# A gated attention block on one core: one table for all engines' orders, banks and places, in place of a recorded schedule that was rearranged

## The chip, the core and the metric

The kernel runs on one core of a Trainium2 chip. Its time is the device time of one execution in microseconds (us); a version is told by the median of its runs. The core's engines run side by side, each through its own list of instructions in order: PE multiplies matrices (PEld loads its weights), ACT computes functions such as the exponential, DVE and POOL compute elementwise, SP issues DMA transfers. ACT and POOL can issue transfers too. An instruction can wait for a semaphore, which other instructions or landed transfers raise; whatever stands behind it on its engine waits with it.

## The reference, cut to what matters

All in bf16; S = 2048 rows, D = 448, 16 heads of 28, F = 1792. The input B_x isn't used.

```python
xn = _layernorm(x)                       # x: (1, 2048, 448)
qkv = xn @ wqkv                          # to q, k, v of (16 heads, 2048, 28)
p = softmax(q @ k.T * 28 ** -0.5)        # for each head, 2048 x 2048
s = (p @ v) @ wo                         # (2048, 448)
g = silu(gelu(xn @ w1 + b1) @ w2 + b2)   # F = 1792 inside
return x + s * g
```

## The kernel before

**Tiles and stages.** The 2048 queries are cut into C = 4 chunks of 512, the heads into G = 4 groups of four; a group's four heads lie in four strips of 32 partitions. A pair of group and chunk is a block (16 of them). In a block, each of 16 tiles of 128 keys gives four score tiles of 128 x 512, one a head, 1024 in all (`qT,kT` in the profile, f32 in a bank of PSUM; the eight banks are the `ring`). A score tile is made into exponentials in one of two ways. ACT takes two or three banks at once through Exp (`P<-ring`, or to places in `h` or `xnT` that are free at the time). Or DVE writes an approximation by integer arithmetic (one pass to uint16 from the bank) and two further terms, which are the first one shifted by a constant (`H` on DVE, two halves `G` on POOL). PE then multiplies the exponentials with V (`P,vaug` and the like), 32 partitions a head, and adds up over the keys in one bank; in the approximate way, each of the terms is multiplied by its own scaled V, and sometimes two shifted terms are added first (on DVE, or by an accumulating DMA that POOL issues) so that PE has one matmul less for each tile. A column of ones in V gives the softmax's sums. At a block's end DVE takes the bank out (`E_sb`), and the reciprocals of the sums make a round trip through DRAM on SP's queue (`rs`, `recs`, then `x_sb<-recs`, the broadcast). Between the score tiles PE does the projections (`xnT,wq`, `xnT,wk`, `wv,xnT`), the MLP (`xnT,w`, `w,h`) and the output. The tail multiplies by g, adds to the copy of x in `out`.

**The start.** `loads` (L1378) issues on SP: x of chunk 0, its first tile alone and then its second (semaphores s_x0t, s_x0), two pieces of wq/wk for head group 0, tiles 1 to 3 of chunk 1 of x (s_x1), wv in two pieces (s_wv), chunks 2 and 3 of x, the remaining columns of wq/wk in four pieces, w1 in two; then two copies of x into `out` (`out_x`), wo, b1, and much later w2 and b2. ACT's queue issues tiles 2 and 3 of chunk 0, two pieces of wq/wk and tile 0 of chunk 1, 448 KB together. Chunk 0 is normalised on DVE and ACT (`p_ln`, `p_ln2`), turned on PE (`ident,h`), projected to q and k (`p_first`), and V of chunk 0 is made in `p_v0` (L1921, 64 matmuls `wv,xnT`), whose last 28 a hook puts behind the first four scores. `p_warm` has PE multiply `E_sb,ident` without use until the scores start; `p_busy` with `filler` (L1720) later adds products with a zero matrix to the bank of the sums where the planner finds PE idle.

**What sets the order.** `schedule` plays all these tasks in a planner in Python with costs and due times; each is recorded as an operation with its needs (`op`, L324). `arrange` (L441) then joins some shifted terms or gives some groups of exponentials from ACT to DVE (`TO`), and takes for PE, ACT, DVE and POOL the operations in an order that the table `ORD` gives as distances. For SP it has no entry: SP keeps the recorded order. `place` gives some turns of a bank another bank (`BANKS`) and derives the waits that follow; `emit_all` (L553) numbers the semaphores and issues waits and operations, an operation's waits one by one. All instructions pass through one line of the helper `_Eng`, so in the profile nearly all show L258 (L381 in the changed kernel), and are told apart by their tiles.

Of the kernel before, what the change touches and what calls it, by code (L numbers as in the profile page):

```python
# [6 lines left out]
dt = mybir.dt  # L7
# [7 lines left out]
ORD = {  # L15
# [39 lines left out]
    ),  # L55
    'ACT': (
# [8 lines left out]
    ),  # L65
    'DVE': (
# [21 lines left out]
TO = ()  # L88
# [10 lines left out]
H = 16  # L99
# [198 lines left out]
class _Kernel:  # L298
# [58 lines left out]
    def add(self, t, need, name):  # L357
# [5 lines left out]
        o.no = name  # L363
        return o

    def to(self, ms, us, at, engines, n, ports):


        K = self
# [2663 lines left out]
```

## Time and profile before

| | |
|---|---|
| median of 3 runs | 410.63 us (409.8 to 410.68) |
| span of the profiled execution | 408.0 us |
| busy PE / ACT / DVE / POOL | 395.1 / 398.1 / 343.5 / 194.8 us |
| mean granted clock of PE | 0.998 |
| first exponential on ACT | 12.58 us |
| end of ACT's last computation | 405.50 us |
| moved by DMA | 17.54 MB |

The page gives no time of the profiled execution other than its span, from the first instruction to the last; the runs' times also hold what lies around it. Rows of a timeline are: start, time from the first start to the last end of the group, engine, line, operation, tiles out<-in, shape, count, and in brackets the idle time before it and what ended that. In the rows by stage stand, behind the stage's length, the busy time and count of PE, PEld, DVE, ACT and POOL, then the granted clock, the mean busy share of the sixteen DMA engines and GB/s. Rows of transfers: tiles, issuing queue, count, KB each, median us from issue to landing.

### The profile page before, as it was taken

What the parts mean: (1) busy time and instruction counts of PE and PEld (TensorE: products, weight loads), DVE (VectorE), ACT (ScalarE), POOL (GpSimd) and SP (SyncE); (2) the same over time, 40 slices, a digit from 0 to 9 for tenths busy, and PEclk for the clock granted to TensorE, in tenths of its full rate; (3) what the DMA queues carried; (4) which work ended last, traced back from release to release, by engine and by line L of the source; (5) the groups of instructions that cost most, each with busy time, mean ns of one, the idle gap of its engine ahead of it and who ended that gap; (6) DMA issues with size and microseconds to landing.
All of it is one profiled execution on the core that took longest, in us unless ns stands there. A gap on an engine that the chain in (4) does not pass through costs nothing.

```text
span 408.0 us, 14601 instructions
## 1 busy us (share of the span) xinstructions
PE 395.1 (97%) x6157; PEld 144.6 (35%) x6157; DVE 343.5 (84%) x596; ACT 398.1 (98%) x409; POOL 194.8 (48%) x221
## 2 busy tenths in 40 slices
PE   6899999999999999999999999999999999999996
PEld 5443233333332333332223444332333323333363
DVE  8967688896679889989898127999998999798976
ACT  5999999999999999999999999999999999999995
POOL 7595457649982563254652231156156013555041
PEclk9999999999999999999999999999999999999999
DMA  8902110000101010100331100220010003200065
GB/s 244 305 2 42 4 31 2 16 20 19 29 3 31 2 25 11 34 2 2 77 116 30 30 3 6 55 53 15 18 34 2 4 31 57 64 20 21 14 114 134
DMA packets 18783, 17.54 MB, mean 43 GB/s; under 512 B 8941, under 2 KB 15421, under 8 KB 18686
## 3 DMA queue, kind: packets, MB, share of 16 engines
q1 hardware_dynamic: 16734, 13.55, 12.0%
q0 software_dynamic: 1008, 2.49, 3.8%
q8 instruction: 48, 0.79, 0.9%
q10 hardware_dynamic: 976, 0.57, 0.5%
q14 instruction: 17, 0.14, 0.1%
HBM read 12.54 MB, written 2.88 MB: 38 GB/s over the span
## 4 chain that ended last, share of the span: by engine, by line
PE 59%; ACT 28%; issue 7%; DVE 4%; DMA 1%; POOL 0%; ACTq 0%; DVEq 0%; POOLq 0%
PE ring L258 59%; ACT P L258 16%; ACT h L258 8%; ACT xnT L258 3%; DVE st L258 1%; DVE h L258 1%; DVE xnT L258 1%; DMA x_sb<-in_A_x_dram 1%; DVE vaug L258 0%; DVE x_sb L258 0%; ACT w L258 0%; DVE qT L258 0%; POOL h L258 0%; DVE mv L258 0%; DVE w L258 0%
## 5 line engine op out<-in xcount | busy, mean ns | idle before, releaser
L258 ACT ACTIVATE P<-ring 128x1024 bf16<-128x1024 f32 (+1 forms) x236 | 253.8, 1246 | 1.0 <-PE ring L258 1.0
L258 PE MATMUL ring<-qT,kT 32*128 32x512 bf16 (+2 forms) x1131 | 131.7, 359 | 4.2 <-ACT P L258 1.0
L258 ACT ACTIVATE h<-ring 128x1024 bf16<-128x1024 f32 (+2 forms) x93 | 101.3, 1204 | 2.0 <-PE ring L258 2.0
L258 PEld LDWEIGHTS ring<-qT,kT 32*128 32x128 bf16 x1131 | 36.3, 91 | 121.8 <-ACT P L258 48.1
L258 DVE TENSOR_SCALAR vaug<-ring 128x512 uint16<-128x512 f32 x92 | 60.8, 683 | 5.5 <-PE ring L258 4.8
L258 PE MATMUL ring<-xnT,w 128*32 128x512 bf16 (+1 forms) x880 | 65.3, 381 | 0.0
L258 PE MATMUL ring<-w,h 128*32 128x448 bf16 x896 | 58.5, 356 | 0.0
L258 PE MATMUL ring<-P,vaug 128*32 128x512 bf16 (+2 forms) x606 | 57.9, 351 | 0.2
L258 POOL TENSOR_TENSOR qT<-x_sb,E_sb 128x512 bf16<-128x512 f32 x15 | 17.4, 1162 | 64.6 <-DMA x_sb<-recs 38.0
L258 ACT ACTIVATE xnT<-ring 128x1024 bf16<-128x1024 f32 (+2 forms) x41 | 47.6, 1199 | 0.5 <-PE ring L258 0.5
L258 POOL TENSOR_TENSOR rc<-rs,mone 128x16 f32<-128x16 bf16 x11 | 33.3, 3023 | 28.7 <-DMA rs<-E_sb 14.6
L258 DVE TENSOR_SCALAR w<-ring 128x512 uint16<-128x512 f32 x52 | 34.5, 683 | 2.0 <-PE ring L258 1.7
L258 PEld LDWEIGHTS ring<-xnT,w 128*32 128x32 bf16 (+1 forms) x880 | 21.7, 96 | 28.0 <-issue 6.6
L258 PEld LDWEIGHTS ring<-w,h 128*32 128x32 bf16 x896 | 19.3, 95 | 24.4 <-issue 14.8
L258 PE MATMUL ring<-h,vaug 128*32 128x512 bf16 x201 | 25.1, 383 | 0.0
L258 PE MATMUL ring<-xnT,wq 128*32 128x512 bf16 (+2 forms) x240 | 22.6, 379 | 0.2 <-DVE w L258 0.2
L258 PEld LDWEIGHTS ring<-P,vaug 128*32 128x32 bf16 x606 | 17.3, 95 | 13.6 <-issue 7.4
L258 PE MATMUL ring<-xnT,wk 128*32 128x512 bf16 (+2 forms) x244 | 21.8, 379 | 0.3 <-DVE xnT L258 0.2
L258 DVE TENSOR_SCALAR h<-ring 128x512 uint16<-128x512 f32 x28 | 18.9, 685 | 3.3 <-PE ring L258 3.0
L258 POOL TENSOR_TENSOR qsq<-qT 128x512 bf16<-128x512 bf16 x12 | 13.0, 1079 | 17.0 <-DVE x_sb L258 13.9
L258 DVE CAST qT<-ring 128x512 bf16<-128x512 f32 x15 | 10.3, 688 | 12.7 <-PE ring L258 12.7
L258 DVE CAST h<-ring 128x512 bf16<-128x512 f32 x24 | 16.5, 688 | 4.8 <-PE ring L258 4.8
(207 smaller groups left out, 616.8 us busy)
## 6 DMA issues: line engine op xcount, KB each, us to landing
x_sb<-recs SPq DMA_DIRECT2D x60, 64.0 KB, 2.1
w<-in_B_w_dram SPq DMA_DIRECT2D x1, 1568.0 KB, 7.3
w<-in_B_w_dram SPq DMA_DIRECT2D x1, 1344.0 KB, 8.7
x_sb<-in_A_x_dram SPq DMA_DIRECT2D x2, 448.0 KB, 6.6
out_dram<-in_A_x_dram SPq DMA_DIRECT2D x2, 448.0 KB, 10.6
out_dram<-h POOLq DMA_DIRECT2D x4, 224.0 KB, 4.6
out_dram<-h SPq DMA_DIRECT2D x7, 112.0 KB, 4.4
xnT<-wq POOLq DMA_DIRECT2D x1, 512.0 KB, 6.6
```

Of the source, the lines that this page charges most:

```text
L258: return lambda *a, **k: f(*[real(x) for x in a], **{n: real(x) for n, x in k.items()})
```

## The change

`ORD`, `TO` and `BANKS` go. A string `PLAN` of 3541 entries holds one order over all engines, SP among them, and with each entry the places it uses: `S5/5` is score tile 5 in bank 5, `X0,1/0,1` is an Exp of tiles 0 and 1 into cells 0 and 1, `A` a pass of DVE's approximation with its unit, `H`/`G` a shift on DVE or POOL, `V` a product with V, `E` the taking out of a block's bank, `P`, `J`, `Q` the parts and the end of a projection, `C` a score tile from a padded copy of q, `R16` the recorded operation number 16 as it is (loads, norms, output), with the banks of its turns. `arrange` drops the filler and the recorded scores, exponentials, products with V and projections, and makes them anew in the table's order; each gets its waits from who wrote or read its bank, cell or unit last. The cells of one Exp can now lie at a stride. The entry `M`, an addition of two shifted terms, exists, and the table has none: the five additions of before (two on DVE, three as DMAs of POOL) are left out, and PE multiplies both terms.

```diff
-ORD = {
-    'PE': (
...
-BANKS = {
...
+PLAN = """
+    R16 R29 R250 R21 R2 R3 R4 R5 R6 R7 R8 R0 R1 R9 R22 R27 R30 R17 R33 R264 R38 R24 R34 R28 R294 R31 R25 R35/6 R32 R36/6 R37/6 R39/6 R18 R40/6 R41/6
...
+    R128 R131 R110/4 R132 R262 R97 R119/4 R116/7 R121/7 R112 R136 R127/7 S0/0 S1/1 S5/5 S3/3 S2/2 R137/6 R129 X0,1/0,1 R124 S4/4 R147/6 S7/1 S6/0
...
 class _Use:
+        self.pos = list(range(base, base + n))
...
     def get(self):
-        i = self.use.base + self.off if self.off is not None else slice(self.use.base, self.use.base + self.use.n)
+        p = self.use.pos
+        i = p[self.off] if self.off is not None else slice(p[0], p[-1] + 1, p[1] - p[0] if len(p) > 1 else 1)
...
     def arrange(self):
-        seq = {}
-        for x in TO:
-            (self.to if len(x) > 2 else self.join)(*x)
-        self.chain_up()
...
-            for d in ORD.get(name, ()):
-                at.append(left.pop(d))
-            seq[E] = [lst[i] for i in at + left]
-        self.place(seq)
-        self.emit_all(seq)
+        K = self
+        K.number()
...
+            if name(o) == "filler.f" or o.kind == "x" or name(o) == "p_expq" and s is None:
+                return "gone"
...
+        plan = [(x[0], *([int(z) for z in y.split(",") if z] for y in x[1:].split("/"))) for x in PLAN.split()]
...
+        for x in plan:
+            t, a, at = x[0], x[1], x[2] if len(x) > 2 else []
+            if t in "SC":
+                o = score(a[0], at[0], t == "C")
+            elif t == "X":
+                bs = [sc[m][1] for m in a]
+                st = bs[1] - bs[0] if len(bs) > 1 else 1
+                src, dst = K.ring[:, bs[0]:bs[-1] + 1:st, :], cells(at)
+                need = [("R", H(sc[m][0])) for m in a]
+                for c in at:
+                    need += room([K.b_P[c]], cell, c)
...
+            elif t == "V":
...
+                if m0 in grouped:
+                    need += [("R", H(p)) for p in ([ap[m0 + k] for k in range(4)] if i == 0 else sh[m0, i][1])]
...
     def emit_all(self, seq):
...
+                most = {}
                 for kind, (s, c) in o.need:
...
                         done[id(p.sem)] = p.cnt
-                        self.prog[E].append(lambda eng, s=p.sem, c=p.cnt: eng.wait_ge(s, c))
+                        most[id(p.sem)] = p
+                for p in most.values():
+                    self.prog[E].append(lambda eng, s=p.sem, c=p.cnt: eng.wait_ge(s, c))
```

What that makes of the two orders that the prediction speaks of most is shown here, a row for each instruction or run of like ones: line, operation, tile out<-tile in, shape, and how many.

SP's queue of before at the start of the program; x_sb and h hold the loaded x and wq/wk, a shape of 128x448 is one tile of 112 KB, 128x1792 a chunk of 448 KB:

```order
L258 DMA x_sb<-in_A_x_dram 128x448 x2
L258 DMA h<-in_A_wqkv_dram 128x2x112
L258 DMA h<-in_A_wqkv_dram 64x2x112
L258 DMA x_sb<-in_A_x_dram 128x1344
L258 DMA wv<-in_A_wqkv_dram 128x3x448
L258 DMA wv<-in_A_wqkv_dram 64x448
L258 DMA x_sb<-in_A_x_dram 128x1792 x2
L258 DMA h<-in_A_wqkv_dram 128x2x336 x3
L258 DMA h<-in_A_wqkv_dram 64x2x336
L258 DMA w1<-in_B_w1_dram 128x3x1792
L258 DMA w1<-in_B_w1_dram 64x1792
L258 DMA out_0_dram<-in_A_x_dram 16x14336 x2
```

SP's queue of the changed kernel, from its sixth load on; the five ahead of these are one tile of x (112 KB), 168 KB of wq/wk, a copy of 448 KB of x to out, and 56 and 28 KB of wq/wk:

```order
L381 DMA x_sb<-in_A_x_dram 128x1792
L381 DMA h<-in_A_wqkv_dram 128x2x336
L381 DMA x_sb<-in_A_x_dram 128x448
L381 DMA w1<-in_B_w1_dram 128x3x1792
L381 DMA x_sb<-in_A_x_dram 128x1344
L381 DMA w1<-in_B_w1_dram 64x1792
L381 DMA x_sb<-in_A_x_dram 128x1792
L381 DMA b1h<-in_B_b1_dram 128x14x1
L381 DMA h<-in_A_wqkv_dram 128x2x336
L381 DMA wv<-in_A_wqkv_dram 128x3x448
L381 DMA h<-in_A_wqkv_dram 64x2x336
L381 DMA wv<-in_A_wqkv_dram 64x448
```

wv moved from the sixth and seventh load to the 15th and 17th, x's tiles 1 to 3 of chunk 1 (128x1344) from the fifth to the tenth, w1's large piece (1344 KB) from the 14th to the ninth, and one copy to out from the end to the third place.

PE of before around the first scores (qT,kT); xnT,wk and qsq,bsel belong to k and q of chunk 0, wv,xnT to its V:

```order
L258 MATMUL ring<-xnT,wk 128x256 x2
L258 MATMUL ring<-qsq,bsel 128x256
L258 MATMUL ring<-xnT,wk 128x256 x2
L258 MATMUL ring<-qsq,bsel 128x256
L258 MATMUL ring<-wv,xnT 32x112 x36
L258 MATMUL ring<-qT,kT 128x512 x4
L258 MATMUL ring<-wv,xnT 32x112 x28
L258 MATMUL ring<-qT,kT 128x512 x2
```

and PE of the changed kernel at that place:

```order
L381 MATMUL ring<-xnT,wq 128x256 x4
L381 MATMUL ring<-csq,bsel 128x1
L381 MATMUL ring<-xnT,wk 128x256 x4
L381 MATMUL ring<-qsq,bsel 128x256 x2
L381 MATMUL ring<-wv,xnT 32x112 x64
L381 MATMUL ring<-qT,kT 128x512 x5
```

The V projection's 28 matmuls that followed the first four scores now stand ahead of all scores, with the other 36.

More of the change, by code (lines that the diff above doesn't have):

```diff
@@ L336, in op @@
         o.sem, o.cnt = h if h else (None, 0)
+        if spec and spec[0] in ("exp", "a", "h", "evac", "last"):
+            for b in writes:
+                self.first_w.setdefault(id(b), ([b.w] if b.w is not None else []) + [x for x in b.r if x is not None])
         o.need = [("X", x) for x in self.pre[E]]
@@ L441, in arrange @@
-    def arrange(self):
-        seq = {}
-        for x in TO:
-            (self.to if len(x) > 2 else self.join)(*x)
-        self.chain_up()
-        for E, name in ((PE, "PE"), (ACT, "ACT"), (DVE, "DVE"), (POOL, "POOL"), (SP, "SP")):
-            lst = [o for o in self.ops if o.E == E]
-            at, left = [], list(range(len(lst)))
-            for d in ORD.get(name, ()):
-                at.append(left.pop(d))
-            seq[E] = [lst[i] for i in at + left]
-        self.place(seq)
-        self.emit_all(seq)
@@ L542, in chain_up @@
-    def chain_up(self):
-        chain = [o for o in self.ops if o.port and o.start is not None]
-        for at, o in sorted(self.put_port[::-1], key=lambda x: -x[0]):
-            chain.insert(at, o)
-        last = {}
-        for o in chain:
-            for E, kind in ((POOL if o.E == DVE else DVE, "P"), (o.E, "Q")):
-                if E in last:
-                    o.need.append((kind, (last[E].sem, last[E].cnt)))
-            last[o.E] = o
+        of = lambda h: K.by_h[(id(h[0]), h[1])]
@@ new lines, in arrange @@
+        kd = {id(o): kind(o) for o in K.ops}
+        writer, unit_at, opens = {}, {}, {}
+        for o in K.ops:
+            if o.spec and o.spec[0] in ("s", "sc", "pv"):
+                for b, (_, h) in zip(o.rd, [x for x in o.need if x[0] == "R"]):
+                    if kd[id(of(h))] in ("rest", "ev"):
+                        writer.setdefault(id(b), {})[(id(h[0]), h[1])] = h
+            if o.spec and o.spec[0] == "h":
+                unit_at.setdefault(o.spec[1], {}).update({o.spec[5]: o.spec[2], o.spec[4]: 0})
@@ new lines, in arrange @@
+        final = {o.spec[1]: o for o in K.ops if o.spec and o.spec[0] == "last"}
+        plan = [(x[0], *([int(z) for z in y.split(",") if z] for y in x[1:].split("/"))) for x in PLAN.split()]
+        ops, seq = {o.no: o for o in K.ops}, {E: [] for E in (PE, ACT, DVE, POOL, SP)}
+        full = {x[1][0] for x in plan if x[0] == "P" and x[1][1] == KT - 1}
+        merged = {x[1][0] for x in plan if x[0] == "M"}
+        grouped = {x[1][0] // 4 * 4 for x in plan if x[0] == "A"}
+        left = [sum(1 for x in plan if x[0] == "V" and x[1][0] // 64 == b) for b in range(NBLK)]
@@ new lines, in through @@
+        def through(p):
+            c, s = kd[id(p)], p.spec
+            if c == "rest" or c == "ev":
+                return [p]
+            if c == "pr":
+                return [evac[s[1]]]
+            if c == "core" and s[0] == "last":
+                return [p]
+            if c == "core" and s[0] in ("s", "sc", "pv"):
+                b = (s[1] if s[0] != "pv" else s[2][0])[0] // 64
+                return [final[b]] if b in final else []
+            return []
+        was = {id(o): list(o.need) for o in K.ops}
@@ new lines, in arrange @@
+        K.ops = [o for o in K.ops if kd[id(o)] == "rest" or o in list(evac.values()) or o in list(final.values())]
+        bank = {i: [] for i in range(NRING)}
+        cell, lane = {}, {}
+        sc, ex, ap, sh, pads, acc, burst, begun, part = {}, {}, {}, {}, {}, {}, {}, {}, set()
+        pr, done, last_pad, port, e1 = {}, set(), [], None, None
+        pad_of = [o for o in K.ops if name(o) == "p_pad" and o.E == SP]
+        shc = [o for o in K.ops if name(o) == "p_pad.f"][0]
+        vs = {o.spec[1:]: o for o in K.ops if o.spec and o.spec[0] == "vs"}
@@ new lines, in new, with take, cells @@
+        def new(E, fn, need, spec, port=False):
+            K.n_new += 1
+            o = K.op(E, fn, (K.evsem[E], 10 ** 6 + K.n_new), 1, (), (), "t", 0.1, 0.05, "", (), port, spec=spec)
+            o.need += need
+            return o
+        def take(i):
+            need = [("A" if p.E != PE else "W", H(p)) for p in bank[i]]
+            bank[i] = []
+            return need
+        def cells(cs):
+            reg, k = K.pslots[cs[0]]
+            n = len(cs)
+            st = cs[1] - cs[0] if n > 1 else 1
+            return reg[:, k:k + st * (n - 1) + 1:st, :]
@@ new lines, in used, with room @@
+        def used(x):
+            return [("A", H(p)) for p in [p for p in x if not p.spec or p.spec[0] not in ("exp", "a")] or x]
+        def room(toks, at, key):
+            if key in at:
+                return used(at[key])
+            need, seen = [], set()
+            for b in toks:
+                for h in first.get(id(b), ()):
+                    for p in through(of(h)):
+                        if id(p) not in seen:
+                            seen.add(id(p))
+                            need.append(("A", H(p)))
+            return need
@@ new lines, in touch, with score @@
+        def touch(u, o):
+            lane[u].append(o)
+            for c in lanes(u):
+                cell[c].append(o)
+        first = K.first_w
+        def score(m, b, pad):
+            b0, j, pc, _, _ = K.pieces(m)
+            g, c = b0 // C, b0 % C
+            tk = K.t_score([m], {m: K.ring[:, b, :]}, [], 1)
+            need = take(b)
+            if pad:
+                (t, _, _, _), = pc
+                fn = lambda eng: _mm(eng, K.ring[:, b, :], K.kT[:, g, 128 * t:128 * t + 128], K.qpad[:, :], True, True)
+                need.append(("R", H(pad_of[b0 - 2])))
+            else:
+                fn = tk.fn
+            for tok in tk.reads:
+                need += [("R", h) for h in writer[id(tok)].values()]
+            o = new(PE, fn, need, ("s", (m,)))
+            if pad:
+                pads.setdefault(b0, []).append(o)
+            bank[b] = [o]
+            sc[m] = (o, b)
+            return o
@@ new lines, in sums, with f, fall @@
+        def sums(b, es, acc):
+            fl = []
+            for kk in range(4):
+                for m, v, f0, src in es:
+                    _, j, pc, _, s = K.pieces(m)
+                    g = b // C
+                    if kk >= len(pc):
+                        continue
+                    t, q0, nq, col = pc[kk]
+                    w = K.vs[:, g % 2, K.vt[g].index(t), j, :] if v else K.vaug[:, t, 4 * g + j, :]
+                    def f(eng, j=j, q0=q0, nq=nq, col=col, src=src, w=w, t=t, f0=f0[kk]):
+                        return eng.matmul(acc[32 * j:32 * j + 32, q0:q0 + nq], w, src[:, col:col + nq] if len(src.shape) == 2 else
+                                          src[:, col // 128:(col + nq) // 128, :], tile_position=(0, 32 * j), start=f0, stop=(t == T - 1),
+                                          skip_group_check=True)
+                    fl.append(f)
+            def fall(eng):
+                ins = None
+                for f in fl:
+                    ins = f(eng)
+                return ins
+            return fall
@@ L1807, in boot, with rest @@
         return self.b_qT[0][1].tw is not None
-    def rest(self, tok, mm, reads, prio, full):
+    def rest(self, tok, mm, reads, prio, full, spec):
         K = self
@@ L1822, in finish @@
         K = self
-        mm, reads, prio, full, tok = a
+        mm, reads, prio, full, tok, spec = a
         t0 = K.now
```

708 lines of the change are left out of this document (513 added, 195 removed), and 70 rows, old and new, of tables (BANKS, ORD).

## The prediction

> **What bounds the kernel now.** I read the page's busy shares first, then ACT's order of time at both ends, then a table by stage, and last the transfers of the start.
>
> ```profile
> span 408.0 us, 14601 instructions
> PE 395.1 (97%) x6157; PEld 144.6 (35%) x6157; DVE 343.5 (84%) x596; ACT 398.1 (98%) x409; POOL 194.8 (48%) x221
> ACT  5999999999999999999999999999999999999995
> ```
>
> ACT is the wall: 398.1 of 408.0 us busy, and only the first and the last slice are below 9. Both ends of its timeline show where the other 9.9 us lie:
>
> ```profile
> 12.58 8.36 ACT L258 ACTIVATE P<-ring 128x1024 bf16<-128x1024 f32 x9 [0.36 <-PE ring L258]
> ...
> 340.80 1.22 ACT L258 ACTIVATE P<-ring 128x1024 bf16<-128x1024 f32 x1
> 341.70 1.66 ACT L258 ACTIVATE xnT<-ring 128x1536 bf16<-128x1536 f32 x1
> 343.03 2.59 ACT L258 ACTIVATE P<-ring 128x1536 bf16<-128x1536 f32 x2
> ...
> 403.22 0.54 ACT L258 ACTIVATE h<-ring 128x448 bf16<-128x448 f32 x1 [0.87 <-PE ring L258]
> 404.95 0.55 ACT L258 ACTIVATE h<-ring 128x448 bf16<-128x448 f32 x1 [1.18 <-PE ring L258]
> ```
>
> The first exponential starts at 12.58, and from there ACT has work without a break until the tail. ACT ends at 405.50, so 2.5 us of the 9.9 lie behind it; the stages give what lies ahead of 12.58:
>
> ```profile
> 0.00:5.00 5.00, 1.51 (x8) 1.11 (x9) 3.48 (x18) 1.95 (x3) 3.38 (x18) 1.00 0.61 155
> 5.00:10.00 5.00, 4.90 (x46) 3.90 (x45) 4.79 (x16) 3.96 (x12) 4.39 (x9) 1.00 1.01 329
> 10.00:15.00 5.00, 4.36 (x99) 2.83 (x96) 4.90 (x16) 4.45 (x11) 3.42 (x8) 1.00 1.07 354
> 15.00:20.00 5.00, 4.51 (x81) 1.76 (x83) 5.00 (x14) 5.00 (x7) 1.76 (x4) 1.00 0.81 279
> 20.00:25.00 5.00, 5.00 (x118) 2.54 (x114) 3.69 (x12) 5.00 (x7) 4.49 (x8) 1.00 0.02 5
> 404.00:408.00 4.00, 0.67 (x8) 0.12 (x8) 1.39 (x4) 0.55 (x1) 0.00 (x0) 0.84 0.28 93
> ```
>
> The fifth number is ACT's: idle 3.05, 1.04 and 0.55 in the first three stages, 4.6 in all. That leaves 9.9 - 2.5 - 4.6 = 2.8 us of idle time inside the run, 2.05 of it the two waits of the tail. Waits shorter than a predecessor's drain don't show as idle (two banks last 1.22, but the next operation starts 0.90 later, at 341.70; behind three banks it starts 1.33 later, 341.70 to 343.03). My sum of all ACT starts at such tight pitches comes to 383.8 of the 389.8 us from 12.58 to the tail's end, so 6.0 us is the most that any order of ACT's work can win back; an estimate. It also follows that a first exponential that comes later by d makes the end later by d, less what of the 6.0 is won.
>
> The last two columns are the second thing to see: for 5 to 15 us the sixteen DMA engines are full (shares 1.01 and 1.07, 329 and 354 GB/s), and at 20 us they fall idle. In that stretch the order of the loads decides when each arrives.
>
> ```profile
> 0.73 0.86 SPq L258 DMA_DIRECT2D x_sb<-in_A_x_dram  x2
> 1.64 1.23 SPq L258 DMA_DIRECT2D h<-in_A_wqkv_dram  x2
> 2.91 0.58 SPq L258 DMA_DIRECT2D x_sb<-in_A_x_dram  x1
> 3.54 0.99 SPq L258 DMA_DIRECT2D wv<-in_A_wqkv_dram  x2
> 4.57 1.06 SPq L258 DMA_DIRECT2D x_sb<-in_A_x_dram  x2
> 5.67 2.42 SPq L258 DMA_DIRECT2D h<-in_A_wqkv_dram  x4
> 8.14 1.46 SPq L258 DMA_DIRECT2D w<-in_B_w_dram  x2
> 9.64 1.23 SPq L258 DMA_DIRECT2D out_dram<-in_A_x_dram  x2
> ```
> ```profile
> w<-in_B_w_dram SPq DMA_DIRECT2D x1, 1344.0 KB, 8.7
> x_sb<-in_A_x_dram SPq DMA_DIRECT2D x2, 448.0 KB, 6.6
> out_dram<-in_A_x_dram SPq DMA_DIRECT2D x2, 448.0 KB, 10.6
> ...
> wv<-in_A_wqkv_dram SPq DMA_DIRECT2D x1, 336.0 KB, 4.2
> ...
> w<-in_B_w_dram SPq DMA_DIRECT2D x1, 224.0 KB, 10.2
> ...
> wv<-in_A_wqkv_dram SPq DMA_DIRECT2D x1, 56.0 KB, 4.4
> ```
>
> Issue plus the last column is the landing. Against the KB queued up to and with each load (SP's, and the 448 KB that ACT's queue issues by 2.7): wv 1428 KB at 7.7; the pair of x chunks 2156 on average at 11.4; w 1344 KB, 4312 at 16.8; w 224 KB, 4536 at 19.1; the pair of copies to out 5208 at 20.5. This line is the price list for the new order.
>
> **The change, part by part.**
>
> *The order on SP's queue* (the largest term). Before, SP was left in program order; now the table orders it too. None of its loads of the start waits for anything.
>
> The two lists of SP's queue in the section on the change show what came of it: w1's 1344 KB and a copy of 448 KB to out stand ahead of both the rest of x's chunk 1 (128x1344) and wv, and so do one and both of x's later chunks of 448 KB. The KB up to each, ACT's 448 counted: x tile 1 of chunk 0 (128x448) 1988, chunk 1 3668, wv 4988. By the line above: tile 1 at 7.7 + 3.7 x 560/728 = 10.5; chunk 1 at 11.4 + 5.4 x 1512/2156 = 15.2; wv at 19.1 + 1.4 x 452/672 = 20.0. For wv, the low end counts bytes by the stages: 4190 KB by 15.00, then 279 a us, gives 17.9, plus 1.4 from moved to landed (w 1344 KB: 4312 KB are moved by 15.4 and landed at 16.8), 19.3; the high end adds 1.5 for the 1792 packets of two bytes of 128x14x1 that now stand ahead of it, 21.6. Who waits is seen on PE and DVE:
>
> ```profile
> 3.49 3.99 PE L258 MATMUL ring<-E_sb,ident 128*128 128x256 bf16 x18 [3.49 <-DVE wk L258]
> ...
> 7.97 0.38 PE L258 MATMUL ring<-E_sb,ident 128*128 128x256 bf16 x2
> 8.19 0.24 PE L258 MATMUL ring<-ones,h 128*128 128x1 bf16 x4
> ...
> 11.31 0.63 PE L258 MATMUL ring<-wv,xnT 128*32 128x112 bf16 x36
> 12.15 0.40 PE L258 MATMUL ring<-qT,kT 32*128 32x512 bf16 x4 [0.22 <-DVE qT L258]
> 12.47 0.53 PE L258 MATMUL ring<-wv,xnT 128*32 128x112 bf16 x28
> ```
> ```profile
> 6.83 0.61 DVE L258 BATCH_NORM_STATS2 st<-x_sb 128x6 f32<-128x448 bf16 x1
> ```
>
> The two lists of PE show the V projection of chunk 0 (wv,xnT) in two pieces around the first scores (qT,kT) before, and in one piece now. All 64 matmuls of wv now stand ahead of the first score, and PE works in order: the first score waits for wv. From wv's landing: 0.63 + 0.53 for the 64, and 0.43 from first score to first exponential (12.15 to 12.58): 20.0 + 1.16 + 0.43 = 21.6. A second chain through DVE comes out close to it: the statistics of x chunk 1 (6.83 in before) still stand ahead of chunk 0's xnT copies and qT, and the first exponential came 12.58 - 6.83 = 5.75 behind them: 15.2 + 5.75 = 20.95. The tile at 10.5 is earlier than both need. So the first exponential comes at 21.6 in place of 12.58: **+9.0** (8.3 to 10.6). Nothing hides it, for ACT's remaining work can't start earlier.
>
> *PE's clock.* The 18 warm-up matmuls took 0.222 us each from 3.49 on; two of the same shape at 7.97 were followed 0.22 later, 0.11 each. PE then ran without a gap. Now it stands mostly idle between the projections of chunk 0 and wv's landing, so it may start the V projection and the first scores at the half rate: 1.16 more for the 64 matmuls, and some of 4 us of scores, against nothing if the idle time doesn't cost the clock (0 to +1.9). I take **+1.0**, since in the tail 0.67 us of PE work in 4 us came with a granted clock of 0.84. The Trainium skill ("TensorE: Matmul & The Clock Gate", Part 1) says that the array starts throttled and needs a busy window of some 3.4 us for the full rate; the warm-up row agrees (3.49 to about 7.3), and by that rule alone this term would be its high end and the sum 421.5.
>
> *The five additions left out.* Two were on DVE, three as accumulating DMAs on POOL's queue:
>
> ```profile
> L258 DVE TENSOR_TENSOR x_sb<-x_sb 128x2048 bf16<-128x2048 bf16 x1 | 1.2, 1212 | 0.0
> L258 POOL DMA_DIRECT2D xnT<-wq x1 | 1.1, 1110 | 12.1 <-DVE xnT L258 12.1
> L258 PE MATMUL ring<-ident,zero 128*32 128x128 bf16 x84 | 2.4, 220 | 0.0
> ```
>
> DVE (84%) is rid of 2 x 1.2, POOL of at most 3 x 1.1 of issue (the row is the longest of its three); neither is the wall, so 0. Each costs a further set of four PV matmuls on PE, 20 in all, about 1.1 us of column time; the 84 filler matmuls that go gave 2.4 us of busy time, of which their 0.22 is mostly drain. Even, 0 +- 1.
>
> *The order of ACT, DVE, PE and POOL, banks and places in the middle.* The counts are the same: 298 operations of two banks and 68 of three on ACT, 248 + 92 + 64 of the bit-trick's passes. Places that are now strided change no element count; on ACT I take 0, up to +2 if a stride costs 0.01 us on each of some 235. What the new order does to ACT's waits can be read from no row: it can win at most 6.0, and can bring waits, among them SP's later queue, where broadcasts of reciprocals now have other loads between them. I take **0** (-4 to +3).
>
> Sum: span 408.0 + 9.0 + 1.0 + 0 = 418.0. The median of the runs is 410.63, 2.6 over this execution's span: **420.6 us**.
>
> **The rivals.** (1) *The loads overtake.* If sixteen engines don't hold to the order of issue, wv's second load, issued at about 9.6 (17 loads at the pace of 0.73 to 10.9), would land its own 4.4 later, 14.0; first exponential 15.6, +3.0. With up to 6.0 won back on ACT: 408.0 + 3.0 - 4 + 2.6 = 409.6, at best 407.6. This ends on the other side once the first exponential comes before 12.58 + 6.0 = 18.6. Against it stands the line of landings, which rises with the KB queued. The Trainium skill ("DMA: Bandwidth & Descriptors", on queues and completion order) says that an engine takes descriptors in ring order while completions across a queue may overtake; that shifts landings between neighbours, not past megabytes. Chance 0.07.
> (2) *The order wins back most of ACT's waits* with the late start: 420.6 - 4.5 = 416.1. For it: 2.05 of idle are in the tail alone, where the order can act. Chance 0.15, inside my range.
> (3) *New waits in the middle*, where PE (97%) or a broadcast of reciprocals behind another load holds ACT up: +3 to +8, 424 to 429. Against it stands that the same work, in another order, let ACT wait 1.0 us in all for PE before its 236 exponentials:
>
> ```profile
> L258 ACT ACTIVATE P<-ring 128x1024 bf16<-128x1024 f32 (+1 forms) x236 | 253.8, 1246 | 1.0 <-PE ring L258 1.0
> ```
>
>  Chance 0.13.
>
> **How the numbers follow.** Forecast 0.65 (417 to 424), rivals 0.07, 0.15 and 0.13. The low end takes wv at 19.3, no clock term and 4 won back: 408.0 + 8.3 - 4 + 2.6 = 414.9, I take 414; the high end 10.6 + 1.9 + 3: 426.1, I take 426.5. A measurement tells 0.2% (0.8 us) from no change. Faster by more than that needs rival 1 with a good order: 0.04; same 0.03; slower 0.93.
>
> **What would show it.** In the profile after: wv's landing near 20, PE's wv,xnT row starting there with a wait for it, ACT's first exponential at 21 to 23.5; then a full ACT, the span ending about as far behind its first exponential as now (395.4 us). Wrong, if the first exponential comes before 18.6, if wv lands before 16, or if the distance from first exponential to the end differs by over 4 us.

## The result, and the profile after

The changed kernel takes **425.22 us** (median of 4 runs, 424.13 to 425.80) against 410.57 before: the ratio is 1.0361, 95% interval 1.0343 to 1.038. The forecast was 420.6 with a range to 426.5. The span of its profiled execution is 422.3 us, 14.3 over the 408.0 of before. Of these, 13.7 lie in ACT's idle time: its busy time is 398.7 us, 0.6 more than before.

The page of the changed kernel, the same lines as shown of before:

```profile
span 422.3 us, 13855 instructions
PE 399.9 (95%) x6093; PEld 145.4 (34%) x6093; DVE 344.0 (81%) x594; ACT 398.7 (94%) x409; POOL 191.2 (45%) x218
ACT  1588999999999999999999999999999999999995
```

ACT's slices now read 1, 5 and 8 at the start. Its timeline (start, duration, group, count, wait ahead of it and what ended that) shows where it waits from the first exponential on:

```profile
23.67 10.19 ACT L381 ACTIVATE P<-ring 128x1024 bf16<-128x1024 f32 x11 [0.58 <-PE ring L381]
35.08 9.52 ACT L381 ACTIVATE P<-ring 128x1024 bf16<-128x1024 f32 x10 [1.22 <-PE ring L381]
...
409.53 6.96 ACT L381 ACTIVATE P<-ring 128x1024 bf16<-128x1024 f32 x7 [0.91 <-PE ring L381]
417.62 0.54 ACT L381 ACTIVATE h<-ring 128x448 bf16<-128x448 f32 x1 [1.13 <-PE ring L381]
419.23 0.54 ACT L381 ACTIVATE h<-ring 128x448 bf16<-128x448 f32 x1 [1.07 <-PE ring L381]
```

The first exponential comes at 23.67 in place of 12.58, 11.1 later. From there to the end are 398.6 us in place of 395.4, 3.2 more: there are new waits of 1.22 at 35.08 and 0.91 at 409.53, which are the two largest parts of it, while the two of the tail are nearly what they were (2.20, before 2.05). So there are two things to explain, 11.1 us at the start and 3.2 behind it.

The start, by stage (columns as before: PE, PEld, DVE, ACT, POOL, clock, DMA share, GB/s):

```profile
5.00:10.00 5.00, 2.70 (x13) 1.60 (x11) 0.00 (x0) 0.00 (x0) 3.17 (x12) 1.00 0.89 278
10.00:15.00 5.00, 1.72 (x15) 1.49 (x15) 2.37 (x9) 3.11 (x11) 0.74 (x1) 1.00 1.03 356
15.00:20.00 5.00, 2.68 (x19) 2.15 (x18) 3.78 (x12) 1.67 (x4) 1.69 (x5) 1.00 0.82 156
20.00:25.00 5.00, 4.82 (x86) 2.69 (x84) 3.18 (x10) 3.26 (x9) 2.64 (x4) 1.00 0.09 23
```

DVE and ACT do nothing between 5 and 10 us, while the transfers run nearly as full as before (a share of 0.89 against 1.01). Three engines say what they wait for; first DVE, then PE, then SP's issues:

```profile
10.57 0.63 DVE L381 BATCH_NORM_STATS2 st<-x_sb 128x6 f32<-128x448 bf16 x1 [6.42 <-DMA x_sb<-in_A_x_dram]
...
15.74 0.63 DVE L381 BATCH_NORM_STATS2 st<-x_sb 128x6 f32<-128x448 bf16 x1 [2.21 <-DMA x_sb<-in_A_x_dram]
...
31.12 2.67 DVE L381 TENSOR_SCALAR h<-x_sb,mv,rstd 128x448 bf16<-128x448 bf16 x2
```
```profile
18.61 0.63 PE L381 MATMUL ring<-xnT,wq 128*128 128x256 bf16 x2
19.04 1.06 PE L381 MATMUL ring<-xnT,wk 128*128 128x256 bf16 x4
...
21.62 0.63 PE L381 MATMUL ring<-qsq,bsel 128*128 128x256 bf16 x2
22.19 1.08 PE L381 MATMUL ring<-wv,xnT 128*32 128x112 bf16 x64
...
33.54 1.15 PE L381 MATMUL ring<-ident,h 128*128 128x128 bf16 x16 [1.53 <-DVE h L381]
```
```profile
7.73 0.44 SPq L381 DMA_DIRECT2D b1h<-in_B_b_dram  x1
8.21 8.45 SPq L381 DMA_DIRECT2D h<-in_A_wqkv_dram  x1
16.70 0.88 SPq L381 DMA_DIRECT2D wv<-in_A_wqkv_dram  x1
17.62 0.63 SPq L381 DMA_DIRECT2D h<-in_A_wqkv_dram  x1
18.29 0.60 SPq L381 DMA_DIRECT2D wv<-in_A_wqkv_dram  x1
```

DVE waits 6.42 us for a tile of x that landed at 10.5, and 2.21 for the rest of chunk 1, landed at 15.7. PE's four matmuls `xnT,wk` take 1.06 us together, where four of that shape took 0.60 before: it runs at half rate from 13 to about 21 us. The clock column shows 1.00 there because this trace's record of the clock begins at 22.5 us only; ahead of that the rate has to be read from the matmuls' own times. PE's row of wv, 64 matmuls at 22.19, has no wait for wv at all. And the load behind the one of 1792 tiny packets (b1h) took 8.45 us to issue, so that wv was issued only at 16.7; it landed at 21.4.

### The profile page after: what moved, and what is told of

The parts are those of the page before. It is cut to its first block, busy times and chain, and to the rows that moved or that the text cites. A ratio compares the mean times of both kernels' runs of the same rounds, so it can differ in the third digit from the quotient of the medians.

```text
span 422.3 us, 13855 instructions
## 1 busy us (share of the span) xinstructions
PE 399.9 (95%) x6093; PEld 145.4 (34%) x6093; DVE 344.0 (81%) x594; ACT 398.7 (94%) x409; POOL 191.2 (45%) x218
## 4 chain that ended last, share of the span: by engine, by line
ACT 49%; PE 34%; DVE 4%; POOL 2%; DMA 1%; issue 1%; SPq 1%; POOLq 0%; DVEq 0%
ACT P L381 40%; PE ring L381 34%; ACT h L381 8%; DVE kT L381 1%; DMA x_sb<-recs 1%; ACT xnT L381 1%; POOL h L381 1%; DVE xnT L381 1%; SPq L381 1%; POOL qT L381 0%; ACT w L381 0%; DVE h L381 0%; POOL wq L381 0%; DMA recs<-rc 0%; DVE w L381 0%
## 5 line engine op out<-in xcount | busy, mean ns | idle before, releaser
L381 ACT ACTIVATE P<-ring 128x1024 bf16<-128x1024 f32 (+1 forms) x299 | 301.4, 1185 | 3.7 <-PE ring L381 3.4
L381 PE MATMUL ring<-P,vaug 128*32 128x512 bf16 (+2 forms) x757 | 66.9, 350 | 0.3 <-DVE kT L381 0.3
L381 ACT ACTIVATE h<-ring 128x1024 bf16<-128x1024 f32 (+2 forms) x52 | 57.9, 1192 | 2.2 <-PE ring L381 2.2
L381 DVE TENSOR_SCALAR x_sb<-ring 128x512 uint16<-128x512 f32 x68 | 45.3, 687 | 7.1 <-PE ring L381 6.4
L381 POOL TENSOR_TENSOR h<-w 128x448 bf16<-128x448 bf16 x13 | 13.9, 1072 | 70.5 <-ACT P L381 26.4
L381 DVE TENSOR_SCALAR h<-ring 128x512 uint16<-128x512 f32 x44 | 29.5, 686 | 3.5 <-PE ring L381 2.8
L381 PEld LDWEIGHTS ring<-w,h 128*32 128x32 bf16 x896 | 19.5, 95 | 25.0 <-issue 15.0
L381 DVE TENSOR_SCALAR w<-ring 128x512 uint16<-128x512 f32 x32 | 21.5, 686 | 7.0 <-PE ring L381 6.6
L381 PEld LDWEIGHTS ring<-P,vaug 128*32 128x32 bf16 x757 | 19.6, 95 | 19.9 <-issue 11.1
L381 ACT ACTIVATE xnT<-ring 128x1536 bf16<-128x1536 f32 (+2 forms) x19 | 23.2, 1238 | 2.3 <-PE ring L381 2.3
L381 DVE TENSOR_SCALAR kT<-ring 128x512 uint16<-128x512 f32 x32 | 21.3, 685 | 2.4 <-PE ring L381 2.3
L381 DVE CAST kT<-ring 128x512 bf16<-128x512 f32 x13 | 9.0, 689 | 16.2 <-PE ring L381 16.1
L381 DVE TENSOR_SCALAR vaug<-ring 128x512 uint16<-128x512 f32 x28 | 18.8, 684 | 2.6 <-PE ring L381 2.4
```

What stands on the lines that cost most here:

```text
L381: return lambda *a, **k: f(*[real(x) for x in a], **{n: real(x) for n, x in k.items()})
```

## The experiments

Each run below is a change of one or two lists at the end of `arrange`, on the changed kernel unless said otherwise. Ratios are to the kernel before, run on the same chip (its medians 409.9 to 410.25).

**e1: the recorded order of the loads back.**

```diff
+        seq[SP][:17] = sorted(seq[SP][:17], key=lambda o: o.no)
         K.emit_all(seq)
```

> The changed kernel with SP's first 17 loads put back into the order in which they were recorded (wv sixth and seventh, w1 and the copy to out behind x); everything else as changed. Theory L (the order of the loads delays the first exponential, and the rest of the change costs about 3 us behind it): first exponential at 12.5 to 13, so about 11 less than 425.2, 414.0 to 415; the distance from it to the end stays 398.6. Rival M (the new order in the middle is made for a late start, or better than before by itself): the distance falls to 395 or less and the time to 410.6 or below; or it grows and the time stays over 417.

Measured: 415.86 (414.94 to 417.64), ratio 1.0144 (1.0116 to 1.0173). Its timeline of ACT:

```profile
13.19 10.19 ACT L381 ACTIVATE P<-ring 128x1024 bf16<-128x1024 f32 x11 [0.48 <-PE ring L381]
24.59 1.02 ACT L381 ACTIVATE P<-ring 128x1024 bf16<-128x1024 f32 x1 [1.22 <-PE ring L381]
26.40 1.02 ACT L381 ACTIVATE P<-ring 128x1024 bf16<-128x1024 f32 x1 [0.79 <-PE ring L381]
27.95 7.56 ACT L381 ACTIVATE P<-ring 128x1024 bf16<-128x1024 f32 x8 [0.52 <-PE ring L381]
```

The first exponential is back at 13.19, and 9.4 of the 14.7 us are gone. The wait of 1.22 stands where it stood, eleven exponentials behind the first, and has two more behind it. The time is a little above what was expected, since the distance to the end grew to 399.9; the cause of that follows with e5.

**e2: the changed kernel's order of loads in the kernel before.**

```diff
+        q = seq[SP]
+        at = [0, 9, 16, 2, 3, 7, 10, 1, 13, 4, 14, 8, 34, 11, 5, 12, 6]
+        seq[SP] = [q[i] for i in at] + [o for i, o in enumerate(q) if i not in at]
         self.place(seq)
```

> The kernel before with SP's first 17 loads put into the changed kernel's order, nothing else changed. Theory L: first exponential at 22.5 to 24, time 410.6 + 10 to 11 = 420.5 to 422, the distance to the end as before (395.4). Rival (the late start needs the new orders on PE and DVE to show, since before has only 36 of the 64 matmuls of wv ahead of its scores): under 419.

Measured: 420.22, ratio 1.0245 (1.0229 to 1.026). ACT in it:

```profile
23.58 18.44 ACT L258 ACTIVATE P<-ring 128x1024 bf16<-128x1024 f32 x20 [1.54 <-PE ring L258]
```

The first exponential is at 23.58 (+11.0), and from there to the end of the span (418.9) are 395.3 us, as in the kernel before (395.4). The order of the loads alone costs 10.0 us by the medians, and in the profiled execution a later first exponential is a later end, us for us. In this kernel, with its own order on PE, the prediction's chain was the last one: PE's wv,xnT row waits 1.17 us for wv.

**e3, e4, e7: which landing is the last that counts.** On SP's queue, wv goes up behind x's chunk 1 (e3), chunk 1's rest goes up ahead of w1 (e4), or both go ahead of w1 (e7):

```diff
+        q = seq[SP]
+        at = [0, 1, 2, 3, 4, 5, 6, 7, 8, 9, 14, 16, 10, 11, 12, 13, 15]   # e3
+        at = [0, 1, 2, 3, 4, 5, 6, 7, 9, 8, 10, 11, 12, 13, 14, 15, 16]   # e4
+        at = [0, 1, 2, 3, 4, 5, 6, 7, 9, 14, 16, 8, 10, 11, 12, 13, 15]   # e7
+        seq[SP][:17] = [q[i] for i in at]
```

> The changed kernel with wv's two loads moved up to right behind the rest of x's chunk 1, from places 15 and 17 to 11 and 12. My prediction's chain (wv's landing, then 64 matmuls, sets the first exponential): wv lands near 16.5 in place of 21.4 and the first exponential comes down by 0.7 or more, to what the chain of x1 allows. Theory X (the chain from x's chunk 1 through DVE and a PE at half rate ends last, wv is just in time): first exponential within 0.3 of 23.67, time 425 +- 0.8.

> The changed kernel with the rest of x's chunk 1 moved ahead of w1's large piece, from place 10 to 9; wv stays where it is. Theory X: x1 lands near 11.4 in place of 15.7, the chain behind it moves up by 1.8 until the tile that lands at 10.5 holds it, and wv's landing at 21.4 becomes the last wait: first exponential 22.5 to 23.0, time 424.1 to 424.6. The prediction's chain through wv alone: first exponential unchanged at 23.7, 425.2.

> The changed kernel with both the rest of x's chunk 1 and wv moved ahead of w1's large piece; nothing else. Theory X (three landings gate in a row: the tile of chunk 0 at 10.5, chunk 1's rest, wv): with both moved they land by 11.5 and 13, the tile at 10.5 is the last, and from it the chain runs partly at half rate: first exponential 19.0 to 20.0, time 421 to 422. Rival (any one of the two is enough, or none): first exponential over 22.

Measured: e3 424.59 (422.59 to 428.64), ratio 1.0335 (1.0309 to 1.0362); e4 426.30 (423.27 to 427.76), 1.0384 (1.034 to 1.0428); e7 424.01, 1.0334 (1.0307 to 1.0362). In e3 wv had landed by 17.7, and the first exponential came at 24.14, no earlier: wv was not the last to count, the chain from chunk 1's rest (landed at 16.2) was. In e4 it was the other way round, as its rows on PE and the stage behind show:

```profile
18.34 0.46 PE L381 MATMUL ring<-qsq,bsel 128*128 128x256 bf16 x2
22.45 1.69 PE L381 MATMUL ring<-wv,xnT 128*32 128x112 bf16 x64 [3.66 <-DMA wv<-in_A_wqkv_dram]
24.07 1.03 PE L381 MATMUL ring<-qT,kT 32*128 32x512 bf16 x5
```
```profile
24.00:26.00 2.00, 2.00 (x16) 0.43 (x8) 1.81 (x5) 1.25 (x2) 0.00 (x0) 0.50 0.00 0
```

The chain of chunk 1 now ends at 18.8, wv is the last wait, as theory X had it, but the first exponential came at 24.75, not at 22.5 to 23: wv landed at 22.4, 1.0 later than in the changed kernel, and after 3.66 us of waiting PE's granted clock was 0.50, so that the 64 matmuls took 1.69 in place of 1.08. A load that came earlier made the kernel no faster. With both up (e7), the first exponential comes at 20.37, a little later than expected (19 to 20); 3.3 us are won there, and only about one is left at the end. Behind it PE's clock was 0.67 and 0.65 in the stages from 30 to 40 us, with waits of ACT of 1.23, 0.79, 0.52 and 1.47.

**e8: e7 with PE kept busy.** The last of the warm-up products is done 49 times, its result not used.

```diff
+        o = [o for o in seq[PE] if o.no == 74][0]
+        o.fn = lambda eng, f=o.fn: [f(eng) for _ in range(49)][-1]
```

> As e7_x1_wv_up, and PE's last warm-up product repeated 48 times more, so that PE computes without a break from 3.5 to about 13 us in place of standing idle from 7.7 on; the products are thrown away. Theory C (PE loses its clock while it stands idle and the chain to the first scores then runs at half rate): the matmuls of the projections at 0.11 in place of 0.21 us, first exponential 1 to 2 us earlier than in e7, time 1 to 2 lower. Rival (the chain is set by DVE and ACT between the matmuls): less than 0.5 earlier.

Measured: 422.16, ratio 1.0292 (1.0252 to 1.0333); the intervals of e7 and e8 overlap, so the gain in time isn't settled by these runs. The first exponential is, 19.08 against 20.37. The same row in e7, then in e8:

```profile
16.29 1.06 PE L381 MATMUL ring<-xnT,wk 128*128 128x256 bf16 x4
```
```profile
15.84 0.60 PE L381 MATMUL ring<-xnT,wk 128*128 128x256 bf16 x4
```

So half rate is what idle time ahead of a chain costs. The first exponential comes 1.3 us earlier although the chain starts 0.3 later: from the statistics of chunk 1's first late tile (13.00 in e7, 13.34 in e8) to the first exponential are 7.37 us in e7 and 5.74 in e8.

**e5: POOL's squares of the weights moved.** This and all that follow on the changed kernel, apart from e12, have e1's order of loads.

```diff
+        q = seq[POOL]
+        late = [o for o in q if o.no in (218, 230)]
+        q = [o for o in q if o not in late]
+        i = [o.no for o in q].index(214) + 1
+        seq[POOL] = q[:i] + late + q[i:]
```

> The changed kernel with the recorded load order (as in e1_loads_back), and with POOL's squares of the weights (128x1344, 2.43 us) and one small copy behind them moved behind the normalising of x's chunk 3, where they stood before. Theory P (they hold the memory port against DVE's normalising of chunk 2, which takes 2.67 us for two operations in place of 0.69; PE then waits 1.53 for it, ACT 1.22 behind that and two more waits, 2.5 in all, while PE runs at a lowered clock): the waits at 24 to 28 us go, the time falls by 2 to 3 from e1's 415.9 to 413 to 414, and the runs spread less. Rival (the waits belong to the order on PE and come back elsewhere): 415.5 to 416.5.

Measured: 412.92 (412.08 to 414.79), ratio 1.0073 (1.0052 to 1.0095), 2.9 under e1. POOL and DVE side by side, first in e1, then in e5:

```profile
20.43 2.43 POOL L381 TENSOR_TENSOR h<-h 128x1344 bf16<-128x1344 bf16 x1
```
```profile
20.63 2.67 DVE L381 TENSOR_SCALAR h<-x_sb,mv,rstd 128x448 bf16<-128x448 bf16 x2
```
```profile
24.74 2.43 POOL L381 TENSOR_TENSOR h<-h 128x1344 bf16<-128x1344 bf16 x1
```
```profile
20.43 0.69 DVE L381 TENSOR_SCALAR h<-x_sb,mv,rstd 128x448 bf16<-128x448 bf16 x2
```

Beside POOL's product of 2.43 us, DVE's two operations took 2.67 in place of 0.69. The transposes of chunk 2 on PE wait for them, and the scores behind those wait too. In e5 ACT runs 21 exponentials from 12.99 on without a break:

```profile
12.99 19.36 ACT L381 ACTIVATE P<-ring 128x1024 bf16<-128x1024 f32 x21 [0.48 <-PE ring L381]
...
398.55 6.96 ACT L381 ACTIVATE P<-ring 128x1024 bf16<-128x1024 f32 x7 [2.18 <-PE ring L381]
```

The two more waits of e1 go with the clock. PE stood idle for 1.53 us in front of the transposes; behind that its granted clock fell to 0.50 for 3.41 us in e1, and stayed at 1.00 in the changed kernel's execution, with the same hole of 1.53. In all these traces the recorded clock changes in steps of 3.41 us or multiples of it, so the rows are cut at those steps. First e1's, then the changed kernel's:

```profile
21.24:24.65 3.41, 1.76 (x22) 0.99 (x18) 3.41 (x9) 2.19 (x4) 2.50 (x4) 1.00 0.00 0
24.65:28.06 3.41, 3.31 (x26) 0.62 (x30) 0.64 (x2) 2.10 (x3) 3.24 (x6) 0.50 0.01 2
```
```profile
29.31:32.72 3.41, 2.70 (x56) 0.97 (x54) 3.37 (x4) 3.41 (x4) 3.35 (x4) 1.00 0.02 5
32.72:36.13 3.41, 2.36 (x32) 1.24 (x36) 3.06 (x9) 2.17 (x3) 2.50 (x5) 1.00 0.00 0
```

In e1 the hole lies in one step, of which PE was busy for 1.76 us; in the changed kernel it is shared by two, busy for 2.70 and 2.36. The other traces with this hole fit: 1.72 to 1.88 us of work in the step were followed by 0.50 in e3, e7 and e12, and 2.08 and 2.14 us were not in e6 and e8. The hole at the tail fits too: 1.11 to 1.68 us were followed by 0.50 in e3, e8 and e12, and 2.02 us were not in e4 and e5. One step of 1.71 us, where the work of e10 ends, was not followed by a lower clock. So a limit of some 1.9 to 2.0 in 3.41 us is an estimate from these traces.

The Trainium skill ("TensorE: Matmul & The Clock Gate", Part 1) says that the window over which the activity is judged runs freely, so that the same program meets it at another point each time; the rows agree with that. The versions with such holes spread over 1.7 to 6 us from run to run, and the kernel before over 1.1 (409.73 to 410.85 in 22 runs). The runs' own mean clocks go with it in e6, whose five runs took 412.94 at 1.0, 413.94 at 0.996 and 415.3 to 416.0 at 0.991 to 0.992. That the clock alone makes the spread is argued, not shown.

**e6: the last chunk's x behind the fourth broadcast.** On SP's queue, two neighbours change places.

```diff
+        q = seq[SP]
+        i, j = [[o.no for o in q].index(n) for n in (2984, 2942)]
+        q[i], q[j] = q[j], q[i]
```

> The changed kernel with the recorded load order (as in e1_loads_back), and with the 448 KB of x for the last chunk's output moved on SP's queue from between the third and the fourth broadcast of the last but one block's reciprocals to behind the fourth. Theory Q (the load of 1.29 us of issue delays the broadcast, POOL's product waits for it, PE for POOL, and ACT waits 0.82 to 0.91 ahead of its last exponentials): that wait shrinks to 0.3 or less, time 0.5 to 0.8 under e1's 415.9. Rival (ACT waits there for the order on PE): no change.

Measured: 415.32 (412.94 to 415.98), ratio 1.0116 (1.0091 to 1.014): 0.5 under e1, inside the spread of both. The trace says more than the time. SP in e5, where the load still stands between the third and the fourth broadcast, then POOL behind it; then the same of e6:

```profile
387.39 1.26 SPq L381 DMA_DIRECT2D x_sb<-recs  x3
388.69 0.42 SPq L381 DMA_DIRECT2D h<-in_A_x_dram  x1
389.15 1.25 SPq L381 DMA_DIRECT2D x_sb<-recs  x1
```
```profile
395.73 1.14 POOL L381 TENSOR_TENSOR qT<-x_sb,E_sb 128x512 bf16<-128x512 f32 x1 [6.68 <-DMA x_sb<-recs]
```
```profile
389.39 1.72 SPq L381 DMA_DIRECT2D x_sb<-recs  x4
```
```profile
394.53 1.16 POOL L381 TENSOR_TENSOR qT<-x_sb,E_sb 128x512 bf16<-128x512 f32 x1 [3.47 <-DMA x_sb<-recs]
```

From the first broadcast's issue to POOL's product were 8.3 us, and are 5.1 now. The 64 KB of the fourth broadcast were queued behind 448 KB. In e6 ACT has no wait at that place; in e5 it had 2.18, in e1 0.82. Where the load stays ahead of the broadcast, this wait has no fixed price: 0.91 in the changed kernel, 2.33 in e4, 2.67 in e3 and 4.65 in e8. The spread has a part here too: e5, with this place alone left, spreads over 2.7 us, and e6, with the hole ahead of the transposes alone left, over 3.0.

**e9: the three together.**

> The changed kernel with the three suspects undone together: the recorded load order, POOL's squares of the weights behind chunk 3's normalising, the last chunk's x behind the fourth broadcast. Sum theory: first exponential at 13.0, no wait at 24 to 28 us, none ahead of the last seven exponentials; span near 409, time 411 to 412, runs spread by no more than 2 us; so what is left of the new order of engines, banks, strided places and additions costs 1 to 1.5 at most. Rival (something else in the table costs 2 or more): over 413.

Measured: 411.34 (410.83 to 412.13 in 10 runs), ratio 1.0029 (1.002 to 1.0038). The span is 409.5 with the first exponential at 13.43, 396.1 from there to the end, and neither wait is left. The runs lie within 1.3 us. So these three moves are 13.9 of the 14.7 us (13.6 by the ratios); the rest of the table, with its strided places, its banks and its additions left out, is 1.1 us slower than the kernel before. Of the 1.5 us that the span is longer than before's, 0.85 lie ahead of the first exponential and 0.7 behind it.

**e10: e9 with five additions of shifted terms put back, all on DVE.** In the table, an entry M behind the last shift of groups 628, 700, 764, 828 and 956, and their products of the second shifted term gone.

```diff
-V700,2/1
+M700
```

> As e9_three_back, with five additions of shifted terms put back in as DVE operations of 1.2 us each (all five on DVE, in five groups with room between their shifts and their products, not the groups of before), and 20 products with V less on PE. Theory: additions and products both lie off ACT's path, so the time is e9's within 0.6. Rivals: 1 or more lower (PE's 20 products were on the path), or 1 or more higher (DVE's added 6 us are).

Measured: 415.08 (414.67 to 415.33), ratio 1.0115 (1.0101 to 1.013): 3.7 slower than e9, against the expectation. What PE waited for from 200 to 400 us (total, times, longest), the row of e10 and then that of e9:

```profile
PE ring L180 <- DVE vaug L180: 2.5, 4, 1.0
```
```profile
PE ring L381 <- DVE vaug L381: 0.2, 1, 0.2
```

ACT waited for PE behind it, one wait of 0.89 and 3.1 in all in that stretch:

```profile
270.95 1.45 ACT L180 ACTIVATE xnT<-ring 128x1536 bf16<-128x1536 f32 x1 [0.89 <-PE ring L180]
```

(The helper's line is 180 in this version.) Six us more work on DVE, 84% busy against 83% in e9, held up PE and so ACT; 20 products less on PE gave nothing that could be seen beside it. The first exponential, ahead of all additions, is 0.57 later than in e9 (14.00), so not all of the 3.7 is theirs. These are not the additions of before, of which three were transfers and stood in other groups. That leaving those out cost or won something by itself was not tried.

**e11: the kernel before with a third of its filler.**

```diff
-                for _ in range(3):
+                for _ in range(1):
                     ins = _mm(eng, acc[:, 0:128], self.zero[:, :], self.ident[:, :], False, True)
```

> The kernel before with a third of its filler matmuls (28 of 84, four in place of twelve at each of seven places). Theory: the filler is hidden and the clock is held by the work itself, 410 within 0.5 and the runs as close as before. Rival (the filler holds PE's clock, and without it the clock falls in places): 1 to 3 higher, wider spread, granted clock under 0.99 in some slice.

Measured: 411.81 (410.02 to 413.45 in 12 runs), ratio 1.0042 (1.0029 to 1.0055), and a spread three times as wide. The profiled execution, with a span of 408.1 and a clock of 1.00, shows none of it. The rival's time and spread came, but not its cause: the mean clock is 0.998 or more in each of the twelve runs, and 1.0 in the slowest. What the filler does for the kernel is open.

**e12: the tiny packets behind wv.**

```diff
+        q = seq[SP]
+        at = [0, 1, 2, 3, 4, 5, 6, 7, 8, 9, 10, 11, 13, 14, 15, 16, 12]
+        seq[SP][:17] = [q[i] for i in at]
```

> The changed kernel with the 3.5 KB load of 1792 packets of two bytes moved from SP's 13th to its 17th place, behind wv's two loads; nothing else. In the changed kernel the load behind it took 8.45 us to issue and wv was issued at 16.7 only. Theory: its packets fill the queue, and the issue stalls until they drain; with it behind, wv is issued by 10 and lands at 19.5 to 20.5 in place of 21.4, and since the chain of x's chunk 1 at half rate ends later, the first exponential stays at 23.5 to 24 and the time at 424 to 426. Rival (the queue is full of bytes whatever is in it): the load behind x's last chunk stalls as long.

Measured: 427.74 (426.28 to 428.87), ratio 1.0425 (1.0406 to 1.0445). SP's issues in it:

```profile
7.92 0.56 SPq L381 DMA_DIRECT2D h<-in_A_wqkv_dram  x1
8.52 0.52 SPq L381 DMA_DIRECT2D wv<-in_A_wqkv_dram  x1
9.09 1.41 SPq L381 DMA_DIRECT2D h<-in_A_wqkv_dram  x1
10.54 0.75 SPq L381 DMA_DIRECT2D wv<-in_A_wqkv_dram  x1
```

The stall of 8.45 us is gone, wv is issued 8 us earlier, and yet lands at 21.2, 0.1 earlier and not at the 19.5 to 20.5 expected: what was queued ahead of it set its landing, not the issue and not the tiny packets. The first exponential comes at 24.05. That the time is 2.5 above the changed kernel's was not expected; the profiled execution has its clock at 0.66 from 35 to 40 and from 410 to 415 us, and ACT's wait ahead of its last exponentials is 3.32. These are the two places that e5 and e6 deal with. That its median is higher than the changed kernel's, with the same holes, is not explained by these four runs.

## Why the prediction was right, and where it was wrong

The direction and the range held, and the largest term was the one named. The likely band of 417 to 424 was missed by 1.2 us. The sum was 4.6 us short: 1.1 at the start, 3.2 behind it, and 0.3 between the span and the median (2.9, forecast 2.6). Step by step:

- **ACT sets the end, and a late first exponential costs its whole delay.** Right: e2 shows 11.0 us at one end and 395.3 against 395.4 from there to the other.
- **The landings by KB queued.** Forecast 10.5, 15.2 and 20.0; landed at 10.5, 15.7 and 21.4. The last is near the high end, 1.5 us of which were for the tiny packets. No run shows that price: with them behind wv it landed at 21.2 (e12). So the range held it by luck, and what makes it 1.2 later than the line is open. Rival 1 (loads overtake) is out, by e12: wv's second load was issued at 10.5 there and landed at 21.2, not at 14.0. In the changed kernel it was issued at 18.3, not at 9.6.
- **The last chain: wv, then 64 matmuls.** Wrong. The chain from x's chunk 1 ended later, since it ran at half rate: from the statistics at 15.74 to the first exponential were 7.9 us, not 5.75 (5.98 for the same rows in e1, 5.74 in e8, where PE ran at full rate). In e3 wv came 3.7 us earlier and nothing moved. The two chains lay so close (21.6 and 20.95 in the forecast) that the term came out nearly right.
- **The clock.** The term of +1.0 was put on wv's matmuls and the first scores, and those ran at nearly full rate (1.08 for the 64, 0.97 in e8). It belonged to the projections ahead of them. e8 puts it at 1.3 in e7's order of loads. In the changed kernel's it is nearer 0.8, by an estimate: at full rate wv would have been the last to land, at 21.4, and 1.5 us behind it, as in e8 from its wv row (17.57) to its first exponential (19.08), come to 22.9 in place of 23.67. Start and clock together were forecast at 10.0 and measured at 11.1.
- **The middle and the tail: 0.** This step failed: the profiled execution shows +3.2. The prediction said that what the new order does to ACT's waits can be read from no row. For two places a part could have been read: POOL's product of 2.43 us stood ahead of chunk 3's normalising in the new order, where DVE normalises chunk 2, and a load of 448 KB stood ahead of the fourth broadcast; loads between the broadcasts the prediction even named, without a price. The lengths and sizes stand in the old trace; how far the product holds DVE up doesn't, for there it ran beside no normalising of DVE. e1 to e5 gives 2.9 for the first, e5 to e9 1.6 for the second; both include what a lower clock cost where one came. Rival 3 (new waits, 424 to 429) is what came on top of the forecast's start.
- **Rival 2, ACT's waits won back.** Out: the tail's two waits are 2.20 us, before 2.05. (The 389.8 us of its bound of 6.0 run from 12.58 to 402.4, where the tail's first wait begins, not to the tail's end.)
- **The filler, priced at even.** The price was for PE's time alone. e11 says that two thirds of it are worth 1.6 us to the kernel before (411.81 against 410.25), by a cause that stays open.
- **The five additions, priced at 0.** Left open for the three on POOL; on DVE five such additions came with 3.7 us in e10, so DVE is nearer the path than "neither is the wall" made it: it must be in time, not only have time.

## What to carry to other kernels

When a table takes over the order of a queue that kept the program's order before, read that queue first: add up the bytes ahead of each load that something waits for, and follow each chain from there with the clock that PE will have after standing idle. Then look in the new order for long operations that moved next to others on a resource both use, and for large transfers ahead of small ones on a queue; their lengths and sizes stand in the old trace, and a run with that one operation moved gives the price. Equal counts on every engine say nothing about either.

## What was not expected of the hardware

- Two operations of DVE that take 0.69 us together took 2.67 beside a POOL product of two inputs of 2.43 us, nearly for as long as that ran (e1 and e5).
- With a load of 3.5 KB in 1792 packets ahead of it, SP's next issue took 8.45 us while the transfers ran full; in its place behind wv it held up none of these loads, and wv's landing changed by 0.1 us (e12).
- A hole of 1.53 us on PE was followed by a granted clock of 0.50 over 3.41 us in the traces of e1, e3, e7 and e12 and of 1.00 in others of nearly the same program (the changed kernel, e6, e8). What went with it was PE's work in the step of 3.41 us that held the hole: 1.72 to 1.88 us, against 2.08 and more. The Trainium skill ("TensorE: Matmul & The Clock Gate", Part 1) speaks of an idle window of some 3.4 us for the return to half rate. The length of the step agrees; but idle time of about half a step was enough here, and the measurement decides.
